# Retention followed by a gated MLP on one core: batch 1's transposes and scalings, and batch 0's copies, put on other engines or in another order

## The chip, the cores and the metric

The kernel runs on one core of one Trainium2 chip, as one launch. The metric is device time in microseconds (us) of that launch. Before the change the median of three runs is 296.65 us (296.54 to 297.62).

The engines are named as in the profile: PE does the matmuls (PEld is its weight load), DVE is VectorE, ACT is ScalarE, POOL is GpSimd, and SP issues nearly all DMAs. Each has a queue of its own; they meet only where one waits for another's result.

## The reference

Inputs: q, k, v of shape (batch 8, heads 8, sequence 576, head dimension 64), and the weights w_in (512 x 2048), w_out (2048 x 512) and beta (2048). All are 32-bit floats.

```python
scores = scale * np.matmul(q, k.transpose(0, 1, 3, 2))          # scale = 1 / sqrt(64)
gamma  = 1.0 - 2.0 ** (-5.0 - np.arange(H))                     # one per head
Dmat   = np.where(rel >= 0, gamma[:, None, None] ** rel, 0.0)   # rel = row - column
x      = np.matmul(scores * Dmat, v)                            # heads joined: 4608 x 512
h      = x @ w_in
g      = h * (1.0 / (1.0 + np.exp(-beta * h)))
out    = g @ w_out
```

## The kernel before, in words

The decay `gamma ** (row - column)` is split in two factors, one on the rows of q (`gq`) and one on the rows of v (`gv`, `gvh`), so that what is left of the decay matrix is a mask of ones and zeros. The sequence is cut in chunks: inside a chunk the masked scores are multiplied out, and what earlier chunks give comes from a running state (k transposed times v). Batches 0 to 7 have 512 of their 576 rows treated as a block of their own; the last 64 rows of every batch are gathered in a ninth block.

Everything is done in bf16 on PE, and so f32 loads are cast or scaled first. For batch 1 these steps are:

- `pre_q(1, n)`, n = 0 to 3: scales a quarter of q into the tile `qs` (line 286, on DVE); `t_q` turns `qs` on PE (L346) and copies it out (L347). For batch 2 and later `pre_q` runs on POOL (L293).
- `o_pre(s, 0, a)`: casts k of span s (half of the 512 rows), heads 4a to 4a+3, into `kn` (L572, POOL). `o_pre(s, 1, a)`: scales v into `vn` (L568, POOL, but DVE for span 0, heads 4 to 7).
- `o_T(s, ...)`: turns `kn` on PE (L583) and copies it out as `kT` (L584), one half on DVE and one on ACT. For span 0 the two halves are in two PSUM tiles, for span 1 they are halves of one tile with tag "mm".
- `first_span`, `second_span`: scores (`o_sc`, L598), masks (L604), and the state's products of kn with vn (`o_st`, L614). `first_out`, `second_out`: the block's output (`o_out`, L647 and L658) and its copies to `xT` (L689). `first_out` also holds `o_T(1, ...)`.

Batch 0 has a path of its own at the start (functions with `s_`): `s_x` copies the output to `xT` (L425) and `s_keep` casts states to `sbd` (L453). `betas_safe` guards beta against zero with three small instructions (L254 to L256) on POOL.

The MLP follows batch by batch: `up` and `ups` (L701, L716) with the activation on ACT, then `down` (L736) with a copy and a store.

Inside the whole kernel each engine issues its instructions in the order in which the program emits them. That order is made by `merged`: `fill` is a list of PE steps of the MLP, and every other step is in a stream with a time, which is a place in that list. `merged` sorts all streams' steps by this time and emits each one ahead of the first fill step whose number isn't smaller.

```python
todo = sorted((x for st in streams for x in st), key=lambda x: x[0])
for n, f in enumerate(fill):
    while todo and todo[0][0] <= n:
        todo.pop(0)[1]()
    f()
```

`d0` is the number of the first down step of batch 0. The streams around the change are these (from lines 923 to 927; only the one with `o_T` is touched by the diff; XB is 2):

```python
[(d0 + 7, F(pre_q, 1, n)) for n in range(4)] + [(d0 + 12.5, F(pre_q, XB, n)) for n in range(4)] + ...
[(d0 + 8, F(o_pre, 0, 0, 0)), (d0 + 8, F(o_pre, 0, 0, 1)), (d0 + 9, F(o_pre, 0, 1, 0)),
 (d0 + 12.7, F(o_T, 0, ("O", "sc"), (dve, act))), (d0 + 12.8, F(o_pre, 0, 1, 1, nc.vector)),
 (d0 + 14, first_span), (d0 + 15.9, first_out)],
[(d0 + 10, F(o_pre, 1, 0, 0)), (d0 + 10, F(o_pre, 1, 0, 1)), (d0 + 12, F(o_pre, 1, 1, 0)), (d0 + 12, F(o_pre, 1, 1, 1)),
```

Of the kernel before, what the change touches and what calls it, by code (L numbers as in the profile page):

```python
# [14 lines left out]
ALU = mybir.AluOpType  # L15
# [4 lines left out]
def kernel(  # L20
# [10 lines left out]
    nc = tc.nc  # L31
    B, H, S, D = q.shape
    d_model = H * D
    d_ff = moe_w_in.shape[1]
    N = B * S
    P = 128
    HP = H // 2
# [4 lines left out]
    PC = P // CB  # L42
    TL = S - MB
    NT = B // 2
    assert MB < S and 2 * TL == P and NT * P == MB
    scale = 1.0 / math.sqrt(D)
# [26 lines left out]
    q_tiles, kv_tiles = {}, {}  # L73
# [79 lines left out]
    gvh = consts.tile([P, CB, H], F32, name="gvh")  # L153
# [10 lines left out]
    for x in range(2):  # L164
        t = causal_span[x * D:(x + 1) * D]
# [17 lines left out]
    beta_sb = consts.tile([P, FO], F32, name="beta_sb")  # L183
    rbeta_sb = consts.tile([P, FO], F32, name="rbeta_sb")
    tiny = rbeta_sb
# [19 lines left out]
    def cast_w_in(g, kos=None, pool=()):  # L205
        t = wts[g]
        f0, fn, rows = pieces[g]
        for ko in kos or range(rows[0].start, rows[-1].stop):
            if ko % 2 == 0 or ko in pool:
                nc.gpsimd.tensor_copy(w_in_sb[:, ko, f0:f0 + fn], t[:, ko])  # L210
                continue
            nc.vector.tensor_copy(w_in_sb[:, ko, f0:f0 + fn], t[:, ko])
# [34 lines left out]
    def betas():  # L247
        pb = psum.tile([P, FO], F32, name="pb", tag="mm", bufs=3)
        nc.tensor.transpose(pb[:], beta_rows[:], ident_f[:FO, :FO])
        nc.scalar.copy(beta_sb[:], pb[:])  # L250

    def betas_safe():

        nc.gpsimd.tensor_tensor(tiny[:], beta_sb[:], beta_sb[:], ALU.mult)  # L254
        nc.gpsimd.tensor_scalar(tiny[:], tiny[:], 1e-24, 1e-12, ALU.is_lt, ALU.mult)
        nc.gpsimd.tensor_tensor(beta_sb[:], beta_sb[:], tiny[:], ALU.add)  # L256

# [2 lines left out]
    def xt(m):  # L262
        if m not in xts:
            xts[m] = xpool.tile([P, HP, CB, P], BF16, name="xT", tag="xT" if m < B else "xTt", bufs=2 if m < B else 1)
        return xts[m]

    state_ps = {}
    batch, pair, live, vns = {}, {}, {}, {}
# [9 lines left out]
    def pre_q(b, n):  # L278

        if n == 0:  # L280
            batch[b] = dict(qs=sb.tile([P, CB, H, D], BF16, name="qs", tag="qs", bufs=2),
                            qT=sb.tile([P, CB, HP, P], BF16, name="qT", tag="qT", bufs=2))
        if b < 2:
            hs, cs = slice(n // 2 * HP, (n // 2 + 1) * HP), slice(n % 2 * 2, n % 2 * 2 + 2)
            for to, hs in [(hs, hs)] if n < 2 or b < QB else turned[1:]:
                nc.vector.tensor_tensor(batch[b]["qs"][:, cs, to], q_tiles[b][:, hs, cs].rearrange("p h i d -> p i h d"),
                                        gq[:, cs, hs].unsqueeze(3).to_broadcast([P, 2, len(range(H)[hs]), D]), ALU.mult)
        else:
            if n % 2:
                return  # L290
            cs = slice(n, n + 2)
            for to, hs in turned:
                nc.gpsimd.tensor_tensor(batch[b]["qs"][:, cs, to], q_tiles[b][:, hs, cs].rearrange("p h i d -> p i h d"),  # L293
                                        gq[:, cs, hs].unsqueeze(3).to_broadcast([P, 2, len(range(H)[hs]), D]), ALU.mult)
# [31 lines left out]
    def heads(t, p):  # L326
        return t[:, 2 * p:2 * p + 2, :].rearrange("p h d -> p (h d)")
# [23 lines left out]
    def half(x):  # L351
        return slice(x * D, (x + 1) * D)

    act, dve = nc.scalar.copy, nc.vector.tensor_copy
    spans = {}

    def span_of(b, s):
        if (b, s) not in spans:
            spans[b, s] = dict(kn=sb.tile([P, 2, H, D], BF16, name="kn", tag="kn", bufs=4),
                               kT=sb.tile([P, 2, HP, P], BF16, name="kT", tag="kT", bufs=4),  # L360
                               vn=sb.tile([P, 2, H, D], BF16, name="vn", tag="vn", bufs=VB), R={})
        return spans[b, s]

    def pre_s(s, j, a):

        w = slice(a * HP, (a + 1) * HP)
        S = span_of(0, s)
        to, src = S["kv"[j] + "n"][:, :, w], span_tiles[0, s, j][:, w].rearrange("p h i d -> p i h d")
        if a == j:
# [36 lines left out]
    def s_O(s, a, tag):  # L406

        if s == 0:
            s_Os[a] = [psum.tile([P, 2, 2, P], F32, name="O", tag=tag, bufs=2) for _ in range(2)]
        for i in range(2):  # L410
            for pl in range(2):
                for j, hh in spread:
                    nc.tensor.matmul(s_Os[a][hh][half(j), s, pl, :], spans[0, s]["vn"][half(hh), i, 2 * (2 * a + pl) + j, :],
                                     spans[0, s]["R"][a][half(hh), j, i, pl, :], start=s == 0 and i == 0 and pl == 0,
                                     stop=i == 1 and s == 0 and hh == 0, skip_group_check=True)
# [8 lines left out]
    def s_x(a, hh, e):  # L424
        e(xt(0)[:, 2 * a:2 * a + 2].rearrange("k p i (s h w) -> k (p i) s h w", s=2, h=2)[:, :, :, hh, :],  # L425
          s_Os[a][hh].rearrange("k s p (i w) -> k (p i) s w", i=CB))
# [20 lines left out]
    def s_keep(a, n, es, bank=None, at=None):  # L447

        ps, at = slice(2 * a, 2 * a + 2), 2 * a if at is None else at
        for j in range(2):  # L450
            st = s_sts[min(n, 1) if bank is None else bank][half(j), at:at + 2, half(j)]
            if n < 3:
                es[j](sbds[n][half(j), ps, half(j)], st)  # L453
            else:
                es[j](ends[0][half(1 - j if a else j), ps], st)
# [104 lines left out]
        return lambda: cross(1), evict  # L560


    def o_pre(s, j, a, e=None):

        w, S, e = slice(a * HP, (a + 1) * HP), span_of(1, s), e or nc.gpsimd
        src = span_tiles[1, s, j].rearrange("p h i d -> p i h d")
        if j:
            e.tensor_tensor(S["vn"][:, :, w], src[:, :, w],  # L568
                            gvh[:, 2 * s:2 * s + 2, w].unsqueeze(3).to_broadcast([P, 2, HP, D]), ALU.mult)
            return  # L570
        for to, hs in turned[1:] if a else turned[:1]:
            e.tensor_copy(S["kn"][:, :, to], src[:, :, hs])  # L572

    def o_T(s, tags, es):

        S = spans[1, s]
        for a in range(2):
            if a < len(tags):
                T = psum.tile([P, 2 // len(tags), 2, 2, P], BF16, name="T", tag=tags[a], bufs=3 if tags[a] == "mm" else 2)
            t = T[:, a if len(tags) == 1 else 0]  # L580
            for i in range(2):
                for pl in range(2):
                    nc.tensor.transpose(t[:, i, pl, :], heads(S["kn"][:, i], 2 * a + pl), ident[:])  # L583
            es[a](S["kT"][:, :, 2 * a:2 * a + 2], t)  # L584

    def o_q(c, r, p):
        return batch[1]["qT"][r, :, p, c * PC:(c + 1) * PC]
# [178 lines left out]
    def F(f, *a):  # L766
        return lambda: f(*a)
# [3 lines left out]

    warm_up(2, MB)
    betas()
    betas_safe()
    pre_q(0, 0)
    pre_q(0, 1)
    t_q(0, 0)
    pre_q(0, 2)
    pre_q(0, 3)
    keep_warm()  # L780
# [33 lines left out]
    s_x(0, 0, act)  # L814
    s_cross(3, 0)
    s_st(1, 1, 0, low)
    s_x(0, 1, act)
    s_keep(1, 0, (dve, dve), 1)
    s_st(1, 0, 1, low)
    s_keep(1, 2, (dve, dve), 0)  # L820
    s_O(0, 1, "sc")
    s_O(1, 1, "sc")
    cast_w_in(0, (0, 1), (1,))
    cast_w_in(1, (0, 1), (1,))
    cast_w_in(0, (2, 3), (3,))
# [23 lines left out]
    d0 = len(fill)  # L849
# [39 lines left out]
    def first_out():  # L889
        evict, st = o_out(0)  # L890
        evict()
        o_T(1, ("mm",), (act, dve))
        o_keep(1, st)
# [12 lines left out]
    def triangles():  # L906
        for t, pattern in zip(tri, ([[1, CB], [CB, TL // CB]], [[1, TL]])):
            nc.gpsimd.memset(t[:], 1.0)
            for x in range(2):
# [12 lines left out]
                (base[2] - 4.5, F(release, 4)), (base[2] + 10, F(release, 4))],  # L922
               [(d0 + 7, F(pre_q, 1, n)) for n in range(4)] + [(d0 + 12.5, F(pre_q, XB, n)) for n in range(4)] + [(d0 + 11.6, F(t_q, 1, 0)), (d0 + 11.6, F(t_q, 1, 1))],
               [(d0 + 8, F(o_pre, 0, 0, 0)), (d0 + 8, F(o_pre, 0, 0, 1)), (d0 + 9, F(o_pre, 0, 1, 0)),
                (d0 + 12.7, F(o_T, 0, ("O", "sc"), (dve, act))), (d0 + 12.8, F(o_pre, 0, 1, 1, nc.vector)),
                (d0 + 14, first_span), (d0 + 15.9, first_out)],
               [(d0 + 10, F(o_pre, 1, 0, 0)), (d0 + 10, F(o_pre, 1, 0, 1)), (d0 + 12, F(o_pre, 1, 1, 0)), (d0 + 12, F(o_pre, 1, 1, 1)),
                (u1 + 3, second_span), (u1 + 12, second_out)]]

# [87 lines left out]
```

## Time and profile before

| | before |
|---|---|
| median of the runs shown | 296.65 us (296.54 to 297.62) |
| the profiled execution's own time | 296.8 us |
| its span, first to last instruction | 295.1 us |
| PE busy | 284.9 us (97%) |
| DVE, ACT, POOL busy | 103.7, 145.7, 110.4 us |
| granted PE clock, mean | 1.000 |
| DMA moved | 53.99 MB, mean 183 GB/s |

Busy time is the sum over an engine's instructions, and idle time of PE inside the span is about 10 us. The profiled execution is 0.15 us over the median of the runs; 1.7 us of it lie outside the span.

### The profile page before, as it was taken

To read this page: it belongs to the slowest core of one execution; us is meant where nothing else is said; L and a number is where in the kernel's file an instruction comes from. 1 tells how busy PE (TensorE), PEld (TensorE's weight loads), DVE (VectorE), ACT (ScalarE), POOL (GpSimd) and SP (SyncE) were. 2 spreads that over 40 slices of the span, in tenths; PEclk is the share of its full clock that TensorE was granted. 3 is DMA by queue.
4 is the path that set the end of the run, shared out by engine and by line. 5 is a ranking of instruction groups with operands and counts; after the bars stand their busy time and mean duration, and the time that the engine had idled before them with its cause. 6 is when DMAs were issued, how large, how long until landed. Compare 5 with 4: busy or idle time off the path is not lost.

```text
span 295.1 us, 7925 instructions
## 1 busy us (share of the span) xinstructions
PE 284.9 (97%) x3373; PEld 149.2 (51%) x3404; DVE 103.7 (35%) x219; ACT 145.7 (49%) x260; POOL 110.4 (37%) x218
## 2 busy tenths in 40 slices
PE   7899998999999999999999999999999999999995
PEld 2554467875544454455445544554554544444443
DVE  6855566505630651055204530354053500110012
ACT  5556536892377334743483347434770167007600
POOL 6956037945904614271319406764322000000000
PEclk9999999999999999999999999999999999999999
DMA  7999999999999699959999949999996110131011
GB/s 229 306 368 384 377 298 262 224 182 252 181 235 245 183 162 235 238 83 162 233 248 197 200 87 273 185 185 220 204 172 117 73 38 0 36 71 38 0 71 71
DMA packets 119938, 53.99 MB, mean 183 GB/s; under 512 B 93648, under 2 KB 112352, under 8 KB 119904
## 3 DMA queue, kind: packets, MB, share of 16 engines
q1 hardware_dynamic: 119872, 53.49, 82.4%
q8 instruction: 26, 0.43, 0.6%
q14 instruction: 8, 0.07, 0.1%
q10 hardware_dynamic: 32, 0.01, 0.0%
HBM read 36.71 MB, written 9.44 MB: 156 GB/s over the span
## 4 chain that ended last, share of the span: by engine, by line
PE 92%; SPq 3%; DMA 2%; issue 1%; POOL 1%; ACT 0%; DVE 0%
PE po L736 42%; PE ph L701 38%; PE ph L716 4%; SPq L102 2%; DMA wt<-in_moe_w_in_dram 2%; PE O L531 2%; PE O L544 2%; PE sc L485 1%; PE st L503 1%; POOL w_in_sb L210 1%; PE sc L598 0%; PE O L647 0%; SPq L84 0%; PE T L346 0%; PE st L614 0%
## 5 line engine op out<-in xcount | busy, mean ns | idle before, releaser
L736 PE MATMUL po<-w_out_sb,gT 128*128 128x512 bf16 (+3 forms) x595 | 125.2, 365 | 2.4 <-issue 2.1
L703 ACT ACTIVATE gT<-ph,beta_sb 128x512 bf16<-128x512 f32 (+1 forms) x143 | 91.1, 646 | 48.4 <-PE ph L701 48.1
L701 PE MATMUL ph<-xT,w_in_sb 128*128 128x512 bf16 (+1 forms) x561 | 113.0, 358 | 0.6
L736 PEld LDWEIGHTS <-gT 128*128 128x128 bf16 x614 | 58.1, 98 | 62.8
L701 PEld LDWEIGHTS <-w_in_sb 128*128 128x128 bf16 x572 | 55.6, 98 | 55.2 <-DVE first L511 0.6
L743 DVE COPY ot<-po 128x512 f32<-128x512 f32 (+2 forms) x33 | 22.2, 672 | 72.6 <-PE po L736 69.8
L293 POOL TENSOR_TENSOR qs<-qn,gq 128x256 bf16<-128x256 f32 (+1 forms) x36 | 26.3, 759 | 35.4 <-DMA qn<-in_q_dram 35.4
L492 DVE TENSOR_TENSOR R<-sc,tri 128x512 bf16<-128x512 f32 x28 | 17.4, 682 | 60.0 <-PE sc L485 58.3
L322 POOL CAST kn<-kvn 128x128 bf16<-128x128 f32 (+1 forms) x72 | 21.0, 331 | 32.7 <-DMA kvn<-in_k_dram 32.7
L300 POOL TENSOR_TENSOR vn<-kvn,gv 128x512 bf16<-128x512 f32 x24 | 25.0, 1045 | 6.4 <-DMA kvn<-in_v_dram 6.3
L559 ACT CAST xT<-O 128x512 bf16<-128x512 f32 x14 | 7.5, 589 | 32.5 <-PE O L544 32.5
L514 ACT CAST sbd<-warm 128x256 bf16<-128x256 f32 x18 | 7.3, 405 | 25.5 <-DVE warm L511 20.7
L716 PE MATMUL ph<-xT,w_in_sb 128*128 128x512 bf16 x55 | 12.9, 379 | 0.2
L511 DVE TENSOR_TENSOR first<-st,warm 128x256 f32<-128x256 f32 x24 | 10.2, 425 | 2.5
L511 DVE TENSOR_TENSOR warm<-st,first 128x256 f32<-128x256 f32 x18 | 7.6, 422 | 9.6 <-PE st L503 8.4
L559 DVE CAST xT<-O 128x512 bf16<-128x512 f32 x14 | 9.0, 685 | 5.4 <-PE O L544 5.4
L719 ACT ACTIVATE gT<-ph,beta_sb 128x512 bf16<-128x512 f32 x14 | 8.6, 687 | 4.2 <-PE ph L716 4.2
L310 POOL TENSOR_TENSOR kn<-tln,gq 128x128 bf16<-128x128 f32 (+1 forms) x12 | 5.7, 472 | 12.6 <-PE ph L701 11.1
L210 POOL CAST w_in_sb<-wt 128x256 bf16<-128x256 f32 (+1 forms) x15 | 8.0, 546 | 5.0 <-DMA wt<-in_moe_w_in_dram 5.0
L716 PEld LDWEIGHTS <-w_in_sb 128*128 128x128 bf16 x56 | 5.3, 98 | 6.4 <-issue 0.5
L514 ACT CAST sbd<-first 128x256 bf16<-128x256 f32 x18 | 7.3, 404 | 2.3 <-DVE first L511 0.3
L572 POOL CAST kn<-kvn 128x256 bf16<-128x256 f32 (+1 forms) x6 | 3.0, 519 | 13.3 <-DMA kvn<-in_k_dram 13.3
(117 smaller groups left out, 174.1 us busy)
## 6 DMA issues: line engine op xcount, KB each, us to landing
qn<-in_q_dram SPq DMA_DIRECT2D x16, 512.0 KB, 5.7
kvn<-in_k_dram SPq DMA_DIRECT2D x32, 256.0 KB, 5.7
kvn<-in_v_dram SPq DMA_DIRECT2D x32, 256.0 KB, 5.4
out_dram<-ot SPq DMA_DIRECT2D x31, 256.0 KB, 3.4
wt<-in_moe_w_out_dram SPq DMA_DIRECT2D x8, 512.0 KB, 9.3
wt<-in_moe_w_in_dram SPq DMA_DIRECT2D x5, 512.0 KB, 9.4
wt<-in_moe_w_in_dram SPq DMA_DIRECT2D x6, 256.0 KB, 6.2
tln<-in_q_dram SPq DMA_DIRECT2D x8, 128.0 KB, 4.5
```

Source lines behind the costliest of these rows:

```text
L293: nc.gpsimd.tensor_tensor(batch[b]["qs"][:, cs, to], q_tiles[b][:, hs, cs].rearrange("p h i d -> p i h d"), gq[:, cs, hs].unsqueeze(3).to_ ...
L300: nc.gpsimd.tensor_tensor(live[i]["vn"], kv_tiles.pop(i)[:, 1], gains(gv, c), ALU.mult)
L322: nc.gpsimd.tensor_copy(kn[:, c % 2, to], t[:, 0, hs])
L492: nc.vector.tensor_tensor(R[x][:, j].rearrange("k c p q -> k (c p) q"), sc[x, j].rearrange("k c p q -> k (c p) q"), mask, ALU.mult)
L511: nc.vector.tensor_tensor(new[:], add, sums[(c - 1) % 2][:], ALU.add)
L514: nc.scalar.copy((sbq[c] if c < NC - 1 else ends[u])[:], new[:])
L559: (nc.scalar.copy if n % 2 else nc.vector.tensor_copy)(x, o)
L701: nc.tensor.matmul(ph, w_in_sb[:, ko, fo * P:(fo + 1) * P], xts[m][:, ko, :, w], start=(ko == 0), stop=(ko == KO - 1))
L703: nc.scalar.activation(gts[m][:, fo, :, w], ph, ACT.Silu, scale=beta_sb[:, fo:fo + 1])
L716: nc.tensor.matmul(phs[f][:], w_in_sb[:, ko, f * P:(f + 1) * P], xts[m][:, ko], start=(ko == 0), stop=(ko == KO - 1))
L736: nc.tensor.matmul(po[:, x:y], gT[:, fo, ms, :], w_out_sb[:, fo, n0 + x:n0 + y], start=(fo == 0), stop=(fo == FO - 1), skip_group_check=m < 2)
L743: (nc.scalar.copy if m == 0 else nc.vector.tensor_copy)(ot, po[:, :nn])
```

## The change

- `betas_safe` runs on DVE and is emitted later, after the last batch 0 states (before: on POOL, right after beta is loaded).
- Batch 0: `s_x(0, 1)` on DVE (before: ACT), which puts it ahead of DVE's state casts; `s_keep(1, 2)` on ACT (before: DVE).
- `pre_q(1, 3)`, two instructions, on POOL (before: DVE).
- `o_pre(0, 1, 1)` is split: two of its four heads on DVE, two on POOL (before: all on DVE). Its place in the streams is the same, d0 + 12.8.
- `o_T` emits the transposes of both halves and then the two copies (before: transposes and copy of one half, then of the other).

```diff
     def betas_safe():
-        nc.gpsimd.tensor_tensor(tiny[:], beta_sb[:], beta_sb[:], ALU.mult)
-        nc.gpsimd.tensor_scalar(tiny[:], tiny[:], 1e-24, 1e-12, ALU.is_lt, ALU.mult)
-        nc.gpsimd.tensor_tensor(beta_sb[:], beta_sb[:], tiny[:], ALU.add)
+        nc.vector.tensor_tensor(tiny[:], beta_sb[:], beta_sb[:], ALU.mult)
+        nc.vector.tensor_scalar(tiny[:], tiny[:], 1e-24, 1e-12, ALU.is_lt, ALU.mult)
+        nc.vector.tensor_tensor(beta_sb[:], beta_sb[:], tiny[:], ALU.add)
...
             for to, hs in [(hs, hs)] if n < 2 or b < QB else turned[1:]:
-                nc.vector.tensor_tensor(batch[b]["qs"][:, cs, to], q_tiles[b][:, hs, cs].rearrange("p h i d -> p i h d"),
+                e = nc.gpsimd if b and n == 3 else nc.vector
+                e.tensor_tensor(batch[b]["qs"][:, cs, to], q_tiles[b][:, hs, cs].rearrange("p h i d -> p i h d"),
...
-    def o_pre(s, j, a, e=None):
+    def o_pre(s, j, a, split=False):
-        w, S, e = slice(a * HP, (a + 1) * HP), span_of(1, s), e or nc.gpsimd
+        S = span_of(1, s)
+        ws = ((nc.gpsimd, slice(a * HP, (a + 1) * HP)),) if not split else ((nc.vector, slice(a * HP, (a + 1) * HP - 2)), (nc.gpsimd, slice((a + 1) * HP - 2, (a + 1) * HP)))
...
         if j:
-            e.tensor_tensor(S["vn"][:, :, w], src[:, :, w],
-                            gvh[:, 2 * s:2 * s + 2, w].unsqueeze(3).to_broadcast([P, 2, HP, D]), ALU.mult)
+            for e, w in ws:
+                e.tensor_tensor(S["vn"][:, :, w], src[:, :, w],
+                                gvh[:, 2 * s:2 * s + 2, w].unsqueeze(3).to_broadcast([P, 2, w.stop - w.start, D]), ALU.mult)
...
     def o_T(s, tags, es):
-        S = spans[1, s]
+        S, ts = spans[1, s], []
...
-            es[a](S["kT"][:, :, 2 * a:2 * a + 2], t)
+            ts.append(t)
+        for a in range(2):
+            es[a](S["kT"][:, :, 2 * a:2 * a + 2], ts[a])
...
     betas()
-    betas_safe()
...
-    s_x(0, 1, act)
+    s_x(0, 1, dve)
     s_keep(1, 0, (dve, dve), 1)
     s_st(1, 0, 1, low)
-    s_keep(1, 2, (dve, dve), 0)
+    s_keep(1, 2, (act, act), 0)
     s_O(0, 1, "sc")
     s_O(1, 1, "sc")
+    betas_safe()
...
-                (d0 + 12.7, F(o_T, 0, ("O", "sc"), (dve, act))), (d0 + 12.8, F(o_pre, 0, 1, 1, nc.vector)),
+                (d0 + 12.7, F(o_T, 0, ("O", "sc"), (dve, act))), (d0 + 12.8, F(o_pre, 0, 1, 1, True)),
```

More of the change, by code (lines that the diff above doesn't have):

```diff
@@ L560, in d_out @@
         return lambda: cross(1), evict
-    def o_pre(s, j, a, e=None):
-        w, S, e = slice(a * HP, (a + 1) * HP), span_of(1, s), e or nc.gpsimd
+    def o_pre(s, j, a, split=False):
+        S = span_of(1, s)
+        ws = ((nc.gpsimd, slice(a * HP, (a + 1) * HP)),) if not split else ((nc.vector, slice(a * HP, (a + 1) * HP - 2)), (nc.gpsimd, slice((a + 1) * HP - 2, (a + 1) * HP)))
         src = span_tiles[1, s, j].rearrange("p h i d -> p i h d")
         if j:
-            e.tensor_tensor(S["vn"][:, :, w], src[:, :, w],
-                            gvh[:, 2 * s:2 * s + 2, w].unsqueeze(3).to_broadcast([P, 2, HP, D]), ALU.mult)
+            for e, w in ws:
+                e.tensor_tensor(S["vn"][:, :, w], src[:, :, w],
+                                gvh[:, 2 * s:2 * s + 2, w].unsqueeze(3).to_broadcast([P, 2, w.stop - w.start, D]), ALU.mult)
             return
         for to, hs in turned[1:] if a else turned[:1]:
-            e.tensor_copy(S["kn"][:, :, to], src[:, :, hs])
+            nc.gpsimd.tensor_copy(S["kn"][:, :, to], src[:, :, hs])
     def o_T(s, tags, es):
-        S = spans[1, s]
+        S, ts = spans[1, s], []
         for a in range(2):
```

## The prediction

> **What bounds the kernel now.** I read the page first, then the waits of PE, the chain of waits between 8 and 52 us, and then the timelines of all engines around the change. The page and the list of PE's waits:
>
> ```profile
> PE 284.9 (97%) x3373; PEld 149.2 (51%) x3404; DVE 103.7 (35%) x219; ACT 145.7 (49%) x260; POOL 110.4 (37%) x218
> ...
> PE T L346 <- DVE qs L286: 1.1, 4, 0.5
> PE T L583 <- ACT kT L584: 0.9, 1, 0.9
> PE st L444 <- POOL vn L372: 0.3, 1, 0.3
> ```
>
> PE is the bound. After its start it stands still for other engines almost nowhere: the four L346 waits are all before 8 us, and the largest single one after that is the 0.9 us at L583, the transposes of `o_T(1)`. So a change gains at most what it takes out of this short list, and loses whatever it makes PE wait. Times from here on are in the span of the profiled execution, which took 296.8 us as a whole (0.15 us over the median of 296.65 us).
>
> The chain shows that one wait:
>
> ```profile
> 47.94 0.64 ACT xT L689 x2
> 48.57 0.50 ACT kT L584
> 49.07 0.04 issue
> 49.11 0.38 PE T L583 x4
> 49.49 0.87 PE ph L867 x8
> ```
>
> PE had done the first four transposes by 48.2 us; the second four go to the same PSUM tile and are held until ACT has copied the first half out, and ACT is busy with `xT` before that.
>
> The rest is decided by POOL's queue, here with DVE's and PE's rows for the scores and state of batch 1's first span:
>
> ```profile
> 43.65 0.81 DVE L568 TENSOR_TENSOR vn<-kvn,gvh 128x512 bf16<-128x512 f32 x1
> ...
> 44.20 0.64 PE L598 MATMUL sc<-qT,kT 64*64 64x128 bf16 x32
> 44.68 0.42 PE L614 MATMUL st<-vn,kn 64*64 64x64 bf16 x16
> ...
> 46.46 2.04 POOL L568 TENSOR_TENSOR vn<-kvn,gvh 128x512 bf16<-128x512 f32 x2
> 49.22 1.04 POOL L293 TENSOR_TENSOR qs<-qn,gq 128x512 bf16<-128x512 f32 x1 [0.71 <-DMA qn<-in_q_dram]
> 50.74 3.34 POOL L293 TENSOR_TENSOR qs<-qn,gq 128x256 bf16<-128x256 f32 x5 [0.48 <-DMA qn<-in_q_dram]
> 54.03 1.76 POOL L322 CAST kn<-kvn 128x256 bf16<-128x256 f32 x6
> ```
>
> L614 at 44.68 is `o_st(0)`: it reads `vn` of all eight heads, and the last of them come from DVE's L568, done at 44.46, only 0.2 us ahead. POOL meanwhile goes through its steps in the order of the streams: the second span's `vn` (d0 + 12), then `pre_q` of batch 2 (d0 + 12.5, the six L293, which wait twice for q to land), and then batch 2's casts (d0 + 13) at 54.03.
>
> **The change part by part.**
>
> *The split of `o_pre(0, 1, 1)`.* Heads 4 and 5 stay on DVE; heads 6 and 7 go to POOL. The step keeps its time, d0 + 12.8, and that was harmless on DVE, where only the copy of d0 + 12.7 stands ahead. On POOL, d0 + 12.8 is behind all of `pre_q(2)` at d0 + 12.5 and just ahead of the casts of d0 + 13. So POOL's half can't start before the last L293 is done: that one ran from 53.47 for 0.61 us, to 54.08. Nothing ahead of it in POOL's queue waits for PE's later work, so this place holds while PE stands still. One L293 of this size, 128x256, took 0.614 to 0.617 us; half of an L568 of 128x512 (1.044 us) would be 0.52. I take 0.61: 54.69. From POOL's end to PE's start I take 0.06 us: at the start of the kernel `vn` L372 ran 11.00 to 12.04 and PE's L444, which waited for it, began at 12.10. PE resumes at 54.75. It would have reached heads 6 and 7, the seventh of the sixteen L614, at 44.77 (44.68 and six steps of 15 ns). PE works in order, and behind the waiting matmul are the rest of batch 0's down step, `first_out` and all else. The delay is 54.75 - 44.77 = **9.98 us**. Bounds: 9.8 with 0.52 us and no overlap lost, 10.4 if POOL takes as long for half as for a whole; the landing of q may move either by 0.4 (the two waits for it were 0.71 and 0.48). What DVE saves, about 0.4 us of the 0.81, nobody waits for.
>
> *PE's clock after that.* Ten idle microseconds of PE don't occur in the trace of before, but its end shows what idling does:
>
> ```profile
> 294.00:294.70 0.70, 0.00 (x0) 0.00 (x0) 0.00 (x0) 0.00 (x0) 0.00 (x0) 1.00 0.00 0
> 294.80:295.05 0.25, 0.00 (x0) 0.00 (x0) 0.00 (x0) 0.00 (x0) 0.00 (x0) 0.50 0.00 0
> ```
>
> These are stretches of time; the third column from the end is the granted clock. The last matmul ended at 291.89, and by 294.80 the clock is at half. So it will be at half at 54.75. How long it stays there no row shows directly: at the start PE's first matmul began at 1.25, and at 5.55 four transposes took 0.40 us, as at 47.81, so full clock came within 4.3 us. Bounds: nothing, if it came back at once, and half of 4.3, 2.15 us. PE's next stretch is the sixteen half-wide L736 (1.69 us at 45.25 in before), a dense one; behind it `first_out` is paced by copies of other engines as well. I take that this stretch runs at half: **1.7 us** lost. [...]
>
> *`o_T`.* In `o_T(0)` the halves are in two tiles and the queues stay as they were: nothing. In `o_T(1)` the second four transposes follow the first four and end near 48.43 instead of 49.49. `first_ups` (L867) needs the `xT` copies (ended by 48.57, its first half by 48.3) and can run from 48.43 to about 49.3 instead of 49.49 to 50.37. The step behind it (L701) takes the PSUM bank of `T` and so waits for both copies: ACT 48.57 to 49.1, then DVE 0.42 us more, to 49.55 (that they follow each other is what the two L382 of one tile showed at 8.67 and 9.07). It starts at 49.55 instead of 50.37: **0.82 us gained**. Bounds: 0.9, the whole wait, and nothing, if some other copy is as late. This is behind the stall, so it stays.
>
> *`pre_q(1, 3)` on POOL.* Two fewer on DVE at 0.42 us each, two more on POOL at 0.62, between q's landing at 40.15 and about 41.4; that pushes the casts of `kn`, begun at 41.18, back by 0.2 to 0.4 us. PE reads the last of them at 43.18 against 42.77 now, so PE waits 0 to 0.1 us. Any such wait is swallowed: PE only comes to the stall later, and the stall ends when POOL does.
>
> *Batch 0.* `xT` by ACT ended at 15.82 and PE's L716 began at 15.87, 0.13 us after the matmuls ahead of it (15.74). With the other half on DVE from 14.9 (its masks end at 14.87) to 15.6, this 0.13 us goes. The casts follow at 15.6 to 16.2 on DVE and 15.3 to 15.9 on ACT, ahead of L421 at 16.6. The gain is before the stall and so is swallowed too. `betas_safe`: POOL loses 2.1 us (5.43 to 7.57), but waited for a DMA of k at 9.00 anyway; DVE gains three instructions of some 0.1 us (its L148 of 128x15 took 0.105) at 16.2, with nothing due until L425 at 17.1 and beta's first reader (L719) at 19.01. Nothing.
>
> *Sum.* 296.8 + 9.98 + 1.7 - 0.82 = 307.7 us for an execution like the profiled one, **307.5 us** for the median. Behind 54 us PE waits in before for nothing but issue (2.1 us in 13 pieces), so there is no wait that could give the lateness back. SP gets one wait: the fourth load of batch 2's k takes the buffer of this `vn` source, and so goes out at 54.7 instead of 53.42; with PE ten microseconds later nobody feels it.
>
> **The rivals.**
>
> 1. *No stall; the gain alone.* If POOL runs its half where DVE ran it, ahead of `pre_q(2)`, `vn` is complete near 44.5 to 44.9 and the change is worth its small gains: 0.82 + 0.13, 295.7 us, within 0.5%. The point that decides is whether POOL's half comes ahead of the first L293 at 49.22. For it: only the order of the queue speaks against it, no data. Against it: the stream's times, and that POOL stood idle from 50.26 to 50.74 for q. Chance 0.06.
>
> 2. *The stall, but the clock costs nothing.* 305.8 us. The end of the trace speaks against it. 0.12.
>
> 3. *The stall, and the clock costs twice what I took*, because it comes back late: 309.2 us. The 4.3 us at the start speak against it. 0.15.
>
> 4. *The lateness is given back in part*, since DMAs, DVE and POOL go on in those ten microseconds and later waits shrink: 300 to 305 us. PE has no such waits behind 54 us to shrink. 0.05.
>
> The forecast itself has 0.62.
>
> **How the numbers follow.** 307.5 us is the likeliest case. The range runs from 305.3 (no clock loss, and q landing 0.4 us sooner) to 309.2 (the longest POOL half and the longest slow clock that the rows allow, or rival 3) and leaves out rivals 1 and 4. A measurement of this kernel can tell about 0.5% (1.5 us) from no change: slower by more than that has 0.93 (all cases but rival 1 and a remnant), within it 0.06, faster 0.01.
>
> **What would show it.** In the changed profile: an L568 on POOL of 128x256 at about 54.1, behind the L293 and ahead of the L322; among PE's waits one of about 10 us at L614, for POOL's `vn` L568; a granted clock of half in windows between about 48 and 58 us; no wait of L583 for L584, and eight L583 in a row; PE's L716 of batch 0 at about 15.75. The prediction is wrong if POOL's L568 of 128x256 stands ahead of 49 us, or if PE's wait is much shorter than ten microseconds. The size of the clock's part is wrong if the sixteen L736 behind the stall take 1.7 us again, or if the clock is still at half in the up steps of batch 1.

## The result and the profile after

The changed kernel takes 307.39 us (median of five runs, 307.25 to 308.56) against 296.71 us of before on the same chip. The ratio is 1.0357, with a 95% interval of 1.034 to 1.0374: slower by 10.7 us. The forecast was 307.5 us. The profiled execution took 307.31 us, with a span of 305.6 us.

The page's line of PE's granted clock, in 40 slices of the span (tenths of full speed, 9 is 90% or more):

```profile
PEclk9999996799999999999999999999999999999999
```

In two slices, from about 46 to 61 us, the clock is below full; in before it was full in all forty. What PE waited for (in total, times, longest, all in us):

```profile
PE st L619 <- POOL vn L571: 8.2, 1, 8.2
PE ph L239 <- DVE warm L132: 1.2, 1, 1.2
PE T L380 <- POOL kn L371: 0.7, 1, 0.7
PE T L380 <- POOL kn L373: 0.5, 2, 0.3
PE ph L706 <- ACT gT L875: 0.5, 1, 0.5
...
```

The 0.9 us wait for `kT`'s copy is gone. Behind the start there are two new ones: 8.2 us for POOL's `vn` (L571; L568 in before), and 0.45 us in the first up step of batch 1. The waits at L380 belong to the start, where the loads of k landed late in this execution. The diff shifts the lines: L614 is now L619, L293 L294, L322 L323, L736 L741, L701 L706, L867 L872, L870 L875.

POOL's and PE's timelines (start, duration, engine, line):

```profile
48.52 1.04 POOL L294 TENSOR_TENSOR qs<-qn,gq 128x512 bf16<-128x512 f32 x1 [0.32 <-DMA qn<-in_q_dram]
49.99 3.34 POOL L294 TENSOR_TENSOR qs<-qn,gq 128x256 bf16<-128x256 f32 x5 [0.43 <-DMA qn<-in_q_dram]
53.28 0.61 POOL L571 TENSOR_TENSOR vn<-kvn,gvh 128x256 bf16<-128x256 f32 x1
53.84 1.69 POOL L323 CAST kn<-kvn 128x256 bf16<-128x256 f32 x6
```

```profile
45.45 0.26 PE L619 MATMUL st<-vn,kn 64*64 64x64 bf16 x6
53.95 0.48 PE L619 MATMUL st<-vn,kn 64*64 64x64 bf16 x10 [8.24 <-POOL vn L571]
54.36 3.59 PE L741 MATMUL po<-w_out_sb,gT 128*128 128x512 bf16 x15
57.88 0.31 PE L663 MATMUL O<-qT,sbd 64*64 64x128 bf16 x8
...
58.81 0.62 PE L586 MATMUL T<-ident,kn 128*128 128x128 bf16 x8
59.35 1.03 PE L872 MATMUL ph<-xT,w_in_sb 128*128 128x256 bf16 x8
60.84 0.60 PE L706 MATMUL ph<-xT,w_in_sb 128*128 128x256 bf16 x4 [0.45 <-ACT gT L875]
```

POOL's half, 0.61 us long, stands behind the six L294 and ahead of the casts. PE does six of the sixteen L619 and then waits for it. The fifteen L741 behind it are one of full width and fourteen of half width. The half-wide ones follow each other every 0.213 us instead of 0.109, and from the first weight load of the fifteen to L663 it takes 3.52 us (54.36 to 57.88) instead of 1.85 (45.02 to 46.87, to L658). In stretches of time (the clock is the third column from the end):

```profile
45.70:47.50 1.80, 0.01 (x1) 0.00 (x0) 1.80 (x4) 0.00 (x0) 1.72 (x4) 1.00 1.05 339
47.60:57.80 10.20, 3.85 (x25) 2.45 (x24) 0.32 (x1) 1.23 (x3) 9.45 (x17) 0.50 1.18 235
57.90:60.00 2.10, 2.10 (x71) 1.94 (x71) 0.81 (x3) 1.66 (x4) 2.10 (x6) 1.00 1.94 203
```

The clock went to half about 1.9 us after PE stopped and came back 3.9 us after PE went on.

So the 10.5 us between the two spans divide like this. Heads 6 and 7 are multiplied at 53.95 instead of 44.77: 9.18. From there to the first L663 it takes 3.93 instead of 2.10 (to L658 at 46.87): 1.83. From there to the up steps behind the second scores it takes 4.30 (62.18) instead of 4.69 (51.56): -0.39. The rest of the span differs by -0.12. Sum: 10.50.

### The profile page after: what moved, and what is told of

It reads as the page before. It is cut to its first block, busy times and chain, and to the rows that moved or that the text cites. A ratio compares the mean times of both kernels' runs of the same rounds, so it can differ in the third digit from the quotient of the medians.

```text
span 305.6 us, 7956 instructions
## 1 busy us (share of the span) xinstructions
PE 290.6 (95%) x3404; PEld 150.3 (49%) x3404; DVE 103.9 (34%) x219; ACT 145.8 (48%) x261; POOL 109.7 (36%) x218
## 4 chain that ended last, share of the span: by engine, by line
PE 83%; DMA 7%; SPq 6%; POOL 2%; DVE 0%; issue 0%; ACT 0%; POOLq 0%
PE po L741 38%; PE ph L706 36%; SPq L102 4%; DMA wt<-in_moe_w_out_dram 3%; DMA kvn<-in_k_dram 2%; DMA qn<-in_q_dram 2%; PE O L532 1%; PE sc L486 1%; PE st L504 1%; PE O L545 1%; SPq L84 1%; POOL qs L294 1%; POOL kn L373 1%; PE st L445 1%; PE O L414 0%
## 5 line engine op out<-in xcount | busy, mean ns | idle before, releaser
L741 PE MATMUL po<-w_out_sb,gT 128*128 128x512 bf16 (+3 forms) x614 | 130.3, 370 | 0.0
L706 PE MATMUL ph<-xT,w_in_sb 128*128 128x512 bf16 (+1 forms) x572 | 113.6, 358 | 0.5 <-ACT gT L875 0.5
L741 PEld LDWEIGHTS <-gT 128*128 128x128 bf16 x614 | 58.9, 99 | 63.5 <-issue 0.3
L706 PEld LDWEIGHTS <-w_in_sb 128*128 128x128 bf16 x572 | 55.7, 98 | 55.8 <-issue 0.8
L323 POOL CAST kn<-kvn 128x128 bf16<-128x128 f32 (+1 forms) x72 | 20.9, 330 | 47.0 <-DMA kvn<-in_k_dram 43.1
L294 POOL TENSOR_TENSOR qs<-qn,gq 128x256 bf16<-128x256 f32 (+1 forms) x36 | 26.3, 758 | 31.8 <-DMA qn<-in_q_dram 31.8
L721 PE MATMUL ph<-xT,w_in_sb 128*128 128x512 bf16 x56 | 12.9, 379 | 0.0
L512 DVE TENSOR_TENSOR first<-st,warm 128x256 f32<-128x256 f32 x24 | 10.2, 425 | 2.5
L619 PE MATMUL st<-vn,kn 64*64 64x64 bf16 x64 | 2.0, 199 | 8.2 <-POOL vn L571 8.2
L721 PEld LDWEIGHTS <-w_in_sb 128*128 128x128 bf16 x56 | 5.2, 98 | 6.3 <-issue 0.5
```

The lines of the kernel that those rows point to most:

```text
L323: nc.gpsimd.tensor_copy(kn[:, c % 2, to], t[:, 0, hs])
L512: nc.vector.tensor_tensor(new[:], add, sums[(c - 1) % 2][:], ALU.add)
L706: nc.tensor.matmul(ph, w_in_sb[:, ko, fo * P:(fo + 1) * P], xts[m][:, ko, :, w], start=(ko == 0), stop=(ko == KO - 1))
L721: nc.tensor.matmul(phs[f][:], w_in_sb[:, ko, f * P:(f + 1) * P], xts[m][:, ko], start=(ko == 0), stop=(ko == KO - 1))
L741: nc.tensor.matmul(po[:, x:y], gT[:, fo, ms, :], w_out_sb[:, fo, n0 + x:n0 + y], start=(fo == 0), stop=(fo == FO - 1), skip_group_check=m < 2)
```

## The experiments

Each kernel was timed against the kernel before on the same chip; ratios are to that. In the diffs, `...` stands for lines left out.

**The split undone.** All of the change, but `vn` of heads 4 to 7 whole on DVE.

```diff
-        ... else ((nc.vector, slice(a * HP, (a + 1) * HP - 2)), (nc.gpsimd, slice((a + 1) * HP - 2, (a + 1) * HP)))
+        ... else ((nc.vector, slice(a * HP, (a + 1) * HP)),)
```

> The changed kernel with one part undone: vn of span 0, heads 4 to 7, whole on DVE again. Theory (POOL's half stands behind batch 2's q scalings and holds PE; the slow clock follows from PE's standstill): both costs go at once, 296.0 to 296.6 us against 296.7 of before, no PE wait for POOL's vn near 45 us, granted clock 1.00 throughout. What is left is the gain of the reordered transposes, 0.3 to 0.8 us, less what the start costs. Rival (another part of the change, the q scaling on POOL or the reordered transposes, carries a good part of the 10.7 us): 298 to 307 us.

Measured: 296.38 us, ratio 0.9983 (0.9973 to 0.9992). Stall and half clock are gone; the clock was full from 5 to 60 us. What is left of the change is worth 0.5 us.

**The split alone**, put into the kernel before together with the new `o_pre` that it needs.

```diff
...
-    (d0 + 12.8, F(o_pre, 0, 1, 1, nc.vector)),
+    (d0 + 12.8, F(o_pre, 0, 1, 1, True)),
```

> The kernel before with the split of vn of span 0, heads 4 to 7, and nothing else of the change. Theory: all of the loss, without the gain of the transposes: 307.4 to 308.2 us; PE waits 8 to 10 us for POOL's vn and the clock falls to half. Rival (the split alone is harmless, it needs the q scaling on POOL as well): 296.7 us.

Measured: 307.81 us, ratio 1.0363 (1.0346 to 1.038). PE waits 8.9 us for POOL's `vn`, and the clock is at half for 10.2 us behind that:

```profile
54.46 0.48 PE L616 MATMUL st<-vn,kn 64*64 64x64 bf16 x10 [8.92 <-POOL vn L570]
```

This one edit makes the whole loss; no other part is needed.

**POOL's half earlier.** The same split, but its POOL half is emitted ahead of span 1's casts.

```diff
...
-    (d0 + 12.8, F(o_pre, 0, 1, 1, True)),
+    (d0 + 12.8, F(o_pre, 0, 1, 1, True, (0,))), (d0 + 9.5, F(o_pre, 0, 1, 1, True, (1,))),
```

> The changed kernel, but POOL's half of the split step is emitted at d0 + 9.5, right behind the vn of heads 0 to 3, and so ahead of span 1's casts and batch 2's q scalings. Theory (only its place in POOL's queue costs): POOL's 128x256 L571 near 44 us, no PE wait of more than 0.3 us there, full clock, 296.0 to 296.7 us. Rival (two engines on one step, or POOL's slower multiplication, cost by themselves): 298 us or more, with PE waiting for POOL's vn.

Measured: 296.52 us, ratio 0.9989 (0.9978 to 1.0001), no wait for `vn`. Only the place in POOL's queue costs. Two engines on one step are no loss here, and no gain that can be measured.

**POOL's half between**, at d0 + 12.4, ahead of batch 2's q scalings but behind all of span 1.

> The changed kernel with POOL's half of the split step emitted at d0 + 12.4: behind span 1's vn, but ahead of batch 2's q scalings. Theory (PE waits exactly as long as POOL's queue takes to reach the half): POOL is done near 48.8 us, PE stands still for about 4 us instead of 8 to 10. Whether the clock falls in 4 us is open: with the clock at half for the first 3 to 4 us behind it, 302.3 us; with the clock left alone, 300.5 us. Rival (the length of the wait comes from q's landing, whatever the order): 307 us.

Measured: 302.11 us, ratio 1.0177 (1.0151 to 1.0204). PE's rows and the clock:

```profile
45.31 0.26 PE L619 MATMUL st<-vn,kn 64*64 64x64 bf16 x6
48.92 0.47 PE L619 MATMUL st<-vn,kn 64*64 64x64 bf16 x10 [3.35 <-POOL vn L571]
49.73 2.83 PE L741 MATMUL po<-w_out_sb,gT 128*128 128x256 bf16 x14 [0.34 <-issue]
52.49 0.31 PE L663 MATMUL O<-qT,sbd 64*64 64x128 bf16 x8
```

```profile
45.60:48.60 3.00, 0.00 (x0) 0.00 (x0) 2.19 (x4) 0.00 (x0) 2.88 (x5) 1.00 1.01 324
48.70:52.00 3.30, 2.74 (x21) 2.12 (x22) 0.00 (x0) 1.24 (x3) 3.09 (x5) 0.50 1.20 230
52.10:53.00 0.90, 0.90 (x42) 0.68 (x43) 0.06 (x1) 0.41 (x1) 0.90 (x3) 1.00 1.10 227
```

In this execution a stop of 3.35 us was enough: the clock fell just before PE went on, and from there to L663 it took 3.57 us against 2.10, 1.5 lost.

**POOL's half later**, at d0 + 13.5, behind six casts more.

> The changed kernel with POOL's half emitted at d0 + 13.5, so that it stands behind batch 2's first six casts of k as well, which took POOL 1.69 us. Theory: PE's wait grows by 1.65 us and the time with it, 309.0 us; the clock's cost stays, since PE stood still long enough already. Rival (some other late step sets the end of the wait): 307.4 us.

Measured: 309.48 us, ratio 1.041 (1.039 to 1.0431), with a wait of 11.1 us. The casts ahead of the half took 1.70 us; by the two ratios (1.041 less 1.0357, of 297 us) the time grew by 1.6 us, and by their intervals this may be 0.8 us more or less. PE's lateness follows POOL's queue. The wait itself is 2.9 us longer than in the changed kernel's trace, since here PE also came to it 0.62 us sooner (45.09) and POOL's first L294 began 0.58 us later (49.10).

**PE kept busy in its wait**, with 72 matmuls whose results are overwritten.

```diff
         st = psum.tile([P, HP, D], F32, name="st", tag="st", bufs=1)
+        for _ in range(72 if c == 0 else 0):
+            nc.tensor.matmul(st.rearrange("p a d -> p (a d)"), ident[:], ident[:].unsqueeze(1).to_broadcast([P, 2, P]),
+                             start=True, stop=True, skip_group_check=True)
```

> The changed kernel with 72 extra matmuls of 128x256 on the identity, into the state's PSUM tile ahead of the products of kn and vn of span 0's first chunk, so that PE works for some 7.8 us of its wait and the clock has no reason to fall. They are overwritten and cost nothing else. Theory (1.7 to 1.8 us of the 10.7 is the half clock behind the wait): PE resumes at the same time, the fifteen half-wide down matmuls take 1.7 us instead of 3.5, and the time is 305.6 us. Rival (the slow stretch isn't paid, since later waits take it up): 307.4 us.

Measured: 311.56 us, ratio 1.0489 (1.0467 to 1.051): slower, against both expectations. The clock stayed full and the half-wide L744 (L736 in before) took 1.69 us again, but later in the chain of waits there are stretches that no engine explains:

```profile
147.02 1.40 issue
...
179.64 2.48 issue
```

These two are 3.9 us in which PE stood still, in the middle of a group of matmuls, for no other engine. What held it there isn't shown. The comparison was spoiled by this, so the next run repeats it with fewer instructions.

**PE kept busy with nine long matmuls** instead of 72 (f32, on the zeroed warm-up tile; the state's tile is made twice as large to hold their output).

```diff
-        st = psum.tile([P, HP, D], F32, name="st", tag="st", bufs=1)
+        st = psum.tile([P, 2 * HP, D], F32, name="st", tag="st", bufs=1)
+        for _ in range(9 if c == 0 else 0):
+            nc.tensor.matmul(st.rearrange("p a d -> p (a d)"), warm[:, :P], warm[:].unsqueeze(1).to_broadcast([P, 2, 256]),
+                             start=True, stop=True, skip_group_check=True)
+        st = st[:, :HP]
```

> The changed kernel kept busy in its wait as in the run with 72 extra matmuls, but with nine f32 matmuls of 128x512 on the zeroed warm-up tile (some 0.85 us each, 7.7 us in all), so that PE's instruction stream is hardly longer. Theory (the half clock costs 1.7 to 1.9 us of the 10.7, and the 5 us lost in the other run come from PE's two standstills of 1.4 and 2.5 us late in it, which belong to its 144 more instructions): no clock of half, the half-wide down matmuls take 1.7 us, no late standstills, 305.5 us. Rival (keeping PE busy for so long costs by itself later on): 309 us or more.

Measured: 305.89 us against 297.19 of before, ratio 1.0299 (1.0281 to 1.0317). PE's rows (each of the nine f32 matmuls stands as two records):

```profile
45.10 7.99 PE L617 MATMUL st<-warm 128*128 128x512 f32 x18
53.02 0.28 PE L623 MATMUL st<-vn,kn 64*64 64x64 bf16 x6
54.31 0.34 PE L623 MATMUL st<-vn,kn 64*64 64x64 bf16 x10 [1.01 <-POOL vn L571]
54.81 1.69 PE L745 MATMUL po<-w_out_sb,gT 128*128 128x256 bf16 x14 [0.16 <-issue]
56.44 0.31 PE L667 MATMUL O<-qT,sbd 64*64 64x128 bf16 x8
```

PE goes on no sooner (54.31), but at full clock, and in place of the two late standstills there is one of 0.45 us (at 92.82). From 54.31 to the first L667 it takes 2.13 us instead of the changed kernel's 3.93 (to L663), so the clock's part of the loss is 1.8 us in the trace. By the time it is 1.7 us, since the ratio is lower by 0.0058; the two intervals allow 1.0 to 2.5, and that difference also holds POOL's half, which came 0.36 us later here, and a shorter wait in batch 1's first up step (below).

**The order of transposes alone**, in the kernel before.

> The kernel before with the new order of transposes and copies alone. Theory of the prediction's sum: PE's 0.9 us wait for the first copy goes and 0.8 us of it is gained: 295.9 us. After the changed kernel's trace, where PE's next up step then waited 0.45 us for the activation of first_ups: 0.4 us gained, 296.3 us. Rival (the copies follow one another and give all of it back): 296.7 us.

Measured: 296.74 us against 297.11, ratio 0.9995 (0.9982 to 1.0007). Time alone doesn't settle it. The profiled execution was the slowest of the twelve (298.22 us), with late first loads and a stretch of half clock from 7.6 to 11.0 us, but what follows lies behind both. In its trace PE does all eight transposes in a row (48.83) and then waits 0.46 us at the up step for the activation of `first_ups`, as in the changed kernel. From the transposes to the second scores it takes 2.55 us against 2.92 in before, so 0.4 us is gained there.

```profile
48.83 0.62 PE L583 MATMUL T<-ident,kn 128*128 128x128 bf16 x8
...
50.85 0.60 PE L703 MATMUL ph<-xT,w_in_sb 128*128 128x256 bf16 x4 [0.46 <-ACT gT L872]
51.38 0.64 PE L600 MATMUL sc<-qT,kT 64*64 64x128 bf16 x32
```

**Batch 1's last q quarter on POOL alone**, in the kernel before.

> The kernel before with the q scaling of batch 1's last quarter on POOL, and nothing else of the change. The prediction's sum: nothing, at most 0.1 us, 296.7 us. After the runs without the split, where POOL took 0.77 us for each of the two while DVE worked beside it and PE waited 0.25 to 0.35 us in the transposes of q: 0.1 to 0.3 us slower than before, with PE's sixteen L347 taking 1.2 to 1.4 us instead of 1.06. Rival (POOL is fast enough for this place): the sixteen take 1.06 us.

Measured: 297.15 us against 297.19, ratio 1.0001 (0.9991 to 1.001). The sixteen transposes of q took 1.18 us against 1.06, so 0.1 us in the trace, and nothing that the time can show. In the kernel without the split, which reaches this place sooner, they took 1.29:

```profile
40.20 1.54 POOL L287 TENSOR_TENSOR qs<-qn,gq 128x256 bf16<-128x256 f32 x2 [11.30 <-DMA qn<-in_q_dram]
```

```profile
40.90 1.29 PE L347 MATMUL T<-ident,qs 128*128 128x128 bf16 x16
```

Before, PE's transposes ran from 41.03 to 42.09; here from 40.90 to 42.19. The 0.13 us that batch 0's edits brought ends here.

**The parts that paid.** Batch 0's edits and the transposes, nothing of batch 1 on POOL, and the second span's scores ahead of the up step that waited.

```diff
...
-                (u1 + 3, second_span), (u1 + 12, second_out)]]
+                (u1 + 2, second_span), (u1 + 12, second_out)]]
```

> The kernel before with the parts that paid, and no work moved to POOL: batch 0's copy and casts on the other engines, beta's guard on DVE, the reordered transposes; and second_span is moved from u1 + 3 to u1 + 2, ahead of the up step that waited 0.45 us for the activation of first_ups. Theory: 0.13 us at the start and 0.37 us of the transposes, both kept, and 0.2 to 0.3 us more of the up step's wait: 295.9 us against 296.7. Rival (the scores then wait as long for DVE's copy of kT, and the start's gain goes in the waits behind it): 296.4 us.

Measured: 296.37 us against 297.05, ratio 0.9976 (0.9964 to 0.9988): 0.7 us faster than before, and 11 us faster than the change.

```profile
48.58 1.03 PE L872 MATMUL ph<-xT,w_in_sb 128*128 128x256 bf16 x8
49.54 0.68 PE L603 MATMUL sc<-qT,kT 64*64 64x128 bf16 x32
50.14 0.44 PE L619 MATMUL st<-vn,kn 64*64 64x64 bf16 x16
50.51 4.54 PE L706 MATMUL ph<-xT,w_in_sb 128*128 128x256 bf16 x40
```

The scores run where PE had stood still, and the up steps follow with no wait. That is the trace's word alone: by the time this kernel can't be told from the one with only the split undone (ratio 0.9983).

## Why the prediction was right, step by step

*The stall.* Its mechanism is shown from four sides: undone, alone, moved earlier and moved later. Its end was foreseen as the end of the sixth L293 plus one POOL instruction of 0.61 us plus 0.06, and so it came (53.28, 0.61, 53.95). Its size was 9.18 us instead of 9.98. The term that was off is the landing of batch 2's q: POOL's first L294 began at 48.52, not 49.22. In the experiments it began between 48.57 and 49.10, with one at 49.62 (the transposes alone, where all was late from the first loads on). In some of them POOL's last wait there was for DVE's `xT` copies or for PE and not for q. The trace of before was on the late side, and 0.4 us of room for the landing was too little. The lower bound was 9.9 by its own sum (54.08 + 0.52 + 0.06 - 44.77), not 9.8. That PE came to this place 0.77 us later than before didn't matter, as foreseen: the stall ends when POOL does.

*The clock.* 1.7 us forecast, 1.83 in the trace, 1.8 by the trace of the run that kept PE busy. The down matmuls carried it, as said, but they were misread: the 1.69 us in before are fourteen half-wide ones, and one of full width ahead of them left no record there. The fifteen took 1.67 us longer (3.52 less 1.85), so the term came out right. The return of the clock 3.9 us behind the stall fits the bound of 4.3 us from the kernel's start. Behind the shorter stop of 3.35 us (the half between) the clock was at half from 48.63 to 52.04, 3.41 us.

*The transposes.* This is the step that failed in size: 0.82 us forecast, 0.39 in the trace. The wait for ACT's copy did go. But the step reckoned that the next up step takes `T`'s PSUM bank and waits for DVE's copy until 49.55. It waits for ACT's activation of `first_ups` instead:

```profile
60.31 0.48 ACT gT L875
60.79 0.04 issue
60.84 0.60 PE ph L706 x4
```

So it shares a bank with that product, and the programs as built say the same. In all of them `T` has bank 1 and the two products of `first_ups` have banks 2 and 0; the up step's tile has bank 1 in before and bank 2 in the changed kernel and in the one with the transposes alone. With another order of instructions it came to another bank. In the two kernels with extra matmuls it has bank 1 again, and there it does wait for DVE's copy (0.19 us). In the one with nine, the stretch from the transposes to the second scores took 2.28 us (57.38 to 59.66), 0.64 less than in before. Moving the scores ahead of that step took the wait away.

*`pre_q(1, 3)`.* Forecast: POOL done at 41.4 and a wait of at most 0.1 us at the casts of `kn`. POOL was done at 41.7, and the wait came one step sooner, in the transposes of q: 0.1 to 0.3 us in the runs without the stall. The duration was mis-sized, 0.62 for 0.77 (below). It was swallowed by the stall all the same.

*Batch 0.* 0.13 us forecast. With the loads landing alike, the first L721 began at 15.73 in the kernel without the split and at 15.87 in before: 0.14. In the changed kernel's profiled execution everything there was 0.8 us late, since its first loads of k landed late (the w_in issues begin at 9.85, not 8.98). The kernel with the transposes alone, whose start is that of before, shows the same (9.96), and the kernel without the split, whose start is the changed one, doesn't (8.96). So it isn't the change.

*The sum.* Against the forecast of 307.7 us for one execution, the parts add up as -0.80 (q's landing), +0.13 (clock), +0.43 (transposes) and -0.12 (rest), which is 307.3, the 307.31 measured. So part of the closeness is luck: two terms were off by 0.4 to 0.8 us with opposite signs. The 2.1 us of "issue" that the sum allowed PE in before are no waits either: that trace has 3373 matmul records for 3404 weight loads, while the changed kernel's has 3404 of both and no such pieces. They are matmuls without a record, which makes the argument that nothing could give the lateness back stronger.

*The rivals.* That POOL's half might run ahead of the q scalings is excluded by the trace. That the clock costs nothing, or twice as much, is excluded by the 1.83 us in it. That the lateness is given back later is excluded too: behind 62 us the two traces differ by 0.12 us.

## What to carry to other kernels

Before a step is put on another engine, list what is ahead of it in that engine's queue at its place in the program, and when each of those gets its data: a small instruction behind one that waits for a DMA is as late as the DMA (here 0.61 us of POOL's work held PE for 8.24 us). The step's place must move with its engine; three fill steps earlier, the same split cost nothing. In these runs a PE standstill of 3.35 us or more was charged twice, once for itself and once for the slow clock behind it (1.5 us behind 3.35, 1.83 behind 8.24). And before a gap called "issue" is read as idle time, compare the number of matmul records with that of weight loads.

## What the runs showed of the hardware that was not expected

- In the changed kernel POOL and DVE both took longer while they scaled f32 tiles at the same time, so engines met at more than each other's results. POOL's 128x256 multiplication took 0.61 us alone (L571 in the changed kernel) and 0.787 (median of the two L287) with DVE beside it; DVE's of that size went from 0.42 to as much as 0.835:

```profile
L287 DVE TENSOR_TENSOR qs<-qn,gq x4: 424/688/835, 38.5 to 40.4; 128x512 bf16<-128x512 f32 x2, 128x256 bf16<-128x256 f32 x2
L287 POOL TENSOR_TENSOR qs<-qn,gq x2: 782/787/792, 40.1 to 40.9; 128x256 bf16<-128x256 f32 x2
```

  In before, batch 2's four L293 of that size on POOL took 0.614 to 0.617 us, and two of them ran beside DVE's masks (L604, 51.20 to 53.68), which read one of their inputs from PSUM. Why the one pair of engines' instructions took longer side by side and the other didn't isn't shown.

- 72 extra matmuls early in PE's stream (from 45.63 us on) were followed by standstills of 1.40 and 2.48 us, 101 and 134 us later (147.02, 179.64), and nine longer ones by one of 0.45 us. The profile puts all three down to "issue", so it names no engine and no DMA for which PE waited. What held PE isn't shown.
- The half clock behind a stop came in pieces of 3.41 us or three times that (3.41 behind a stop of 3.35 us, 10.24 behind stops of 8.2, 8.9 and 11.1 us), and it began 1.9 to 4.1 us after PE stopped. It also came without such a stop: in three of the profiled executions (the split alone, the half between, the transposes alone; mean granted clocks 0.978, 0.989 and 0.994) the clock was at half for 3.41 us from 7.6 to 8.1 us on, though PE's longest wait since its first matmul had been 0.7 us. What lowered it there isn't shown; in before it stayed full. In the kernel with the transposes alone:

```profile
7.00:7.50 0.50, 0.36 (x4) 0.18 (x4) 0.50 (x1) 0.50 (x1) 0.00 (x0) 1.00 1.16 316
7.70:10.90 3.20, 2.95 (x28) 1.36 (x28) 0.98 (x2) 0.37 (x1) 2.10 (x3) 0.50 1.14 292
11.10:12.00 0.90, 0.66 (x13) 0.37 (x11) 0.90 (x2) 0.67 (x2) 0.90 (x1) 1.00 1.17 294
```
